# Forgetting attention and a bilinear FFN in one kernel: decay by a broadcast row and a DVE pass instead of by matmuls

## The chip, the cores and the metric

One core of a Trainium2 chip. The engines are TensorE (PE, with its weight loads as PEld), VectorE (DVE), ScalarE (ACT), GpSimd (POOL) and SyncE (SP), which issues most of the DMAs. The metric is device time in microseconds of one execution, the median of several runs. The profile is of one further execution.

## The reference

```python
# q, k, v: [8, 8, 576, 64]   f: [8, 8, 576]   fp32
scores = matmul(q, k^T) / sqrt(64)
log_f  = log(clip(f, 0.0001, 1.0))
cum    = cumsum(log_f, axis=-1)
decay  = cum[..., :, None] - cum[..., None, :]
scores = where(causal, -1e9, scores + decay)
attn   = softmax(scores)
x      = matmul(attn, v)         # then [8, 8, 576, 64] -> [4608, 512]
out    = ((x @ w_a) * (x @ w_b)) @ w_out     # w_a, w_b: [512, 1536], w_out: [1536, 512]
```

The term `cum[..., :, None]` is the same for a whole row, so the softmax takes it away again. Only `-cum[..., None, :]`, one value for each column, has to be added to the scores.

## The kernel before, in words

The work is a list of operations (class `Op`), each with an engine or several to choose from, a planned duration, what it depends on, a priority and the ring buffers that it takes. `schedule()` is a planner: it gives each operation an engine and a planned start, and the program is written out in that order. So each engine's queue has a fixed order, made when the kernel is built, and each waits in order for its semaphores.

Attention runs over `t`, a batch b (8) and a pair of heads pr (4), 32 in all. For a pair the queries come in blocks of 128 rows, `i` from 0 to 3, and a last one of 64 rows, `i` = 4, with both heads under each other in the 128 partitions. `groups = [(1, 0), (2,), (3,), (4,)]` says which blocks share a pair of PSUM banks (tile `sc`, two buffers).

For each pair:

- `qk_group` (matmuls at L463): q times k into `sc`; then the matrix `ones16` times `crs`, which adds the decay row: `crs` holds the row in two fp16 halves in two partitions per head; then `low` times `neg64`, the causal mask.
- `do_max` (L502, DVE): the negated maximum of each row of both heads of a block, from PSUM, into `st`.
- `do_exp` (L527, L531, ACT): the exponential of `sc` with that bias, from PSUM, into the fp16 tiles `PA` (blocks 0 to 2) and `PB` (blocks 3 and 4), with the row sum beside it.
- `do_recip` (L538, L540, DVE), then `do_norm` (L548, POOL): scaling of `PA` and `PB` by the reciprocal of the sum.
- `do_tr`: a DMA transpose of `PA` and `PB` on SP's queue (in batch 0 by PE and an eviction: `pe_tr`, L564), then `do_pv` and `do_pv4` (L588, L601, PE), then copies into `xT` (L608, L612, DVE).

`batch_inputs` loads q, k and v by head (L273, 256-byte pieces), casts them to fp16 (L265, L267; mostly on POOL from batch 1 on) and transposes q, k and the 64-row tail: with PE (`pe_path`, L300) for the batches in `PEB`, with DMA transposes for the others. `load_cr` loads `crs` of a batch from `cum_d`, a scratch in DRAM that was written once at the start.

`weights` loads the three weight matrices in 36 pieces of 128x512 fp32 into the ring `wl` by SP and casts each to fp16 on DVE or POOL (L451).

The FFN (`ffn`) follows in chunks of 512 tokens, two of 256 at the start: `psa` and `psb` (L732), a copy (L263, ACT), a product (L743, DVE), `pso` (L752), a copy (L263, L267) and a store (L762). A chunk needs the attention of all the batches that its tokens lie in; the planner puts the matmuls of earlier chunks between those of later pairs.

Of the kernel before, what the change touches and what calls it, by code (L numbers as in the profile page):

```python
# [25 lines left out]
def kernel(  # L26
# [34 lines left out]
    ones16 = perm.tile([128, 128], FP16, tag="ones16", name="ones16")  # L61
    cone = perm.tile([BH, S], FP16, tag="cone", name="cone")
# [3 lines left out]
    def constants():  # L66
        nc.gpsimd.memset(warm, 1.0)
        nc.gpsimd.memset(cone, 1.0)
        make_identity(nc, ident16)
        nc.gpsimd.memset(ones16, 0.0)  # L70
# [3 lines left out]
        for h in range(2):  # L74
            nc.gpsimd.memset(ones16[64 * h:64 * h + 2, :], 1.0)
            nc.gpsimd.affine_select(out=neg64[HP[h], :], in_=neg64[HP[h], :],
                                    compare_op=mybir.AluOpType.not_equal, fill=NEGBIG, base=0,
                                    pattern=[[-1, 64]], channel_multiplier=1)
            for half in range(2):
                x = low[half][HP[h], :]  # L80
                nc.gpsimd.affine_select(out=x, in_=x, compare_op=mybir.AluOpType.is_gt, fill=0.0,
                                        base=64 * half, pattern=[[-1, 128]], channel_multiplier=1)

    def paddings():
        for i in range(2):
            nc.gpsimd.memset(PB[i][:, 12, 64:128], 0.0)
            nc.gpsimd.memset(nv[i][64:128, NSB - 1, :, :], 0.0)
        nc.gpsimd.memset(crs[1], 0.0)
# [3 lines left out]
    wa16 = [perm.tile([128, DF], FP16, tag=f"wa16_{i}", name=f"wa16_{i}") for i in range(4)]  # L92
    wb16 = [perm.tile([128, DF], FP16, tag=f"wb16_{i}", name=f"wb16_{i}") for i in range(4)]
    wout16 = [perm.tile([128, DM], FP16, tag=f"wout16_{i}", name=f"wout16_{i}") for i in range(12)]
    nv = [perm.tile([128, NSB, H, D], FP16, tag=f"nv{i}", name=f"nv{i}") for i in range(2)]
    crs = [perm.tile([128, NP, S], FP16, tag=f"cr{i}", name=f"cr{i}") for i in range(2)]
    PB = [perm.tile([128, 13, 128], FP16, tag=f"PB{i}", name=f"PB{i}") for i in range(2)]

    RING = {"wl": 4, "n32": 4, "n16": 2, "n16t": 1, "nv": 2, "cr": 2, "qT": 2, "kT": 2, "tT": 2,
            "PA": 3, "PB": 2, "PTA": 3, "PTB": 2, "st": 6, "ht": 14, "a16": 3, "osb": 2,  # L100
            "sc": 2, "pv": 1, "ff": 3}
    wl_pool = pool("wl", RING["wl"])
# [9 lines left out]
    dram = pool("scr", 1, space=bass.MemoryType.DRAM)  # L112
# [7 lines left out]
    BACKLOG = 1.0  # L120
    PKT = {256: 0.021, 512: 0.031, 1024: 0.051, 2048: 0.095}

    class Op:


        def __init__(self, eng, dur, fn, deps=(), prio=0.0, land=None, mode=None, name="", bulk=False):
# [3 lines left out]
            self.bulk = bulk  # L130
# [12 lines left out]
    def schedule():  # L143
# [12 lines left out]
        def ready(o, e):  # L156
            t = 0.0
# [4 lines left out]
            for tag, _ in o.takes:  # L162
                lv = lives[tag]
                if len(lv) >= RING[tag]:
                    for u in lv[-RING[tag]]:
# [5 lines left out]
        while len(order) < len(ops):  # L171
            best = None
            for e, lst in pending.items():
                cand = None
                for o in lst:
# [3 lines left out]
                    at = max(r, free[e])  # L179
                    if o.bulk:  # L180
                        at = max(at, dma_free - BACKLOG)
                    if cand is None or at < cand[0] - 1e-9:
                        cand = (at, at + o.durs[e], o, e)
                        if at <= free[e] + 1e-9:
                            break
                if cand and (best is None or cand[0] < best[0] - 1e-9
# [11 lines left out]
            free[e] = at + dur  # L198
# [15 lines left out]
    T = {}  # L214


    cum_d = dram.tile([2, BH, S], FP16, tag="cum_d", name="cum_d")
    cw = {}

    def f_load(_):  # L220
        for n in ("f", "l", "c"):
            cw[n] = wl_pool.tile([128, 576], FP32, tag="wl", name=f"cum_{n}")
        cw["f"], cw["l"] = cw["f"][0:BH, 0:S], cw["l"][0:BH, 0:S]
        cw["c"] = cw["c"][0:BH, :].bitcast(FP16).rearrange("p (c s) -> p c s", c=2)
        nc.sync.dma_start(out=cw["f"], in_=f.rearrange("b h s -> (b h) s"))

    def warm_table(func):
# [3 lines left out]
    o_z = Op("DVE", 1.5, lambda _: nc.vector.memset(crs[0], 0.0), prio=-300)  # L231
    o_w = Op("ACT", 1.4, warm_table(LN), [], prio=-300)
    o_f = Op("SP", 0.55, f_load, prio=-300, land=0.6)
    wl_users = [take(o_f, "wl") for _ in range(3)]
# [4 lines left out]
        out=cw["f"], data0=cone, data1=cw["l"], initial=0.0, op0=MUL, op1=SUB), [o2], prio=-300)  # L239
    o4 = Op("DVE", 0.45, lambda _: nc.vector.tensor_copy(out=cw["c"][:, 0, :], in_=cw["f"]), [o3], prio=-300)  # L240
    o5 = Op("DVE", 0.75, lambda _: nc.vector.tensor_tensor(out=cw["c"][:, 1, :], in0=cw["f"],
                                                           in1=cw["c"][:, 0, :], op=SUB), [o4], prio=-300)
    o6 = Op("SP", 0.55, lambda _: nc.sync.dma_start(out=cum_d.rearrange("c r s -> r c s"), in_=cw["c"]), [o5],
            land=0.6, prio=-300)
    o_e = Op("ACT", 1.4, warm_table(EXP), [o2], prio=-300)
    for u in wl_users:
        u.extend([o1, o2, o3, o4, o5, o6])
# [4 lines left out]
    cr_op, cr_users, kq_users, kq_ops, tail_op, v_ops, v_users = {}, {}, {}, {}, {}, {}, {}  # L252
# [88 lines left out]
    def load_cr(b):  # L341
        for h in range(2):
            nc.sync.dma_start(
                out=crs[b % 2][64 * h:64 * h + 2, :, :],
                in_=cum_d[:, b * H:b * H + H, :].rearrange("c (p t) s -> t c p s", t=2)[h])
# [8 lines left out]
    PEB = (0, 1)  # L354
    PEP = (0,)

    def batch_inputs(b, base):
# [3 lines left out]
        o = Op("SP", 0.6, lambda _: load_cr(b), [o6, o_z] + ([o_p] if b else []) + gate(0), prio=base - 60, land=0.1)  # L361
        cr_users[b] = take(o, "cr")
        cr_op[b] = o
# [70 lines left out]
    def weights(base):  # L434
        items = []
        for j in range(3):
            for i in range(4):
                for nm, src, dst in (("a", moe_w_a, wa16), ("b", moe_w_b, wb16)):
                    cols = slice(512 * j, 512 * j + 512)
                    items.append(((nm, j), src[128 * i:128 * i + 128, cols], dst[i][:, cols]))  # L440
        for i in range(12):
            items.append((("o", i), moe_w_out[128 * i:128 * i + 128, :], wout16[i][:, :]))
        for n, (key, src, dst) in enumerate(items):
            def ld(_, n=n, src=src):
                T[("wl", n)] = wl_pool.tile([128, 576], FP32, tag="wl", name="wl")
                nc.sync.dma_start(out=T[("wl", n)][:, 0:512], in_=src)

            l = Op("SP", 0.55, ld, prio=base + 0.8 * n, land=packets(128, 2048), name=f"ldw{key[0]}{key[1]}", bulk=True)
            u = take(l, "wl")
            c = Op(None, {"DVE": 0.5, "POOL": 0.65},  # L450
                   lambda e, n=n, dst=dst: VEC[e].tensor_copy(out=dst, in_=T.pop(("wl", n))[:, 0:512]),  # L451
                   [l], prio=base + 0.8 * n, name=f"caw{key[0]}{key[1]}")
            u.append(c)
            w_ops.setdefault(key, []).append(c)


    def qk_group(t, g):
# [7 lines left out]
        if g == 3:  # L465
            for r in HP:
                mm(c[r, 0, :], tT[r, pr, 64:128], kT[r, 0:4, pr, :], start=True)
            for r in HP:
                mm(c[r, 1, 0:64], tT[r, pr, 64:128], tT[r, pr, 0:64], start=True)
            for bank, col, n in ((0, 0, 512), (1, 512, 64)):  # L470
                for r in HP:
                    mm(c[r, bank, 0:n], ones16[r, 0:64], crs[b % 2][r, pr, col:col + n], stop=(bank == 0))
# [12 lines left out]
        for i in groups[g]:  # L485
            for h, r in enumerate(HP):
                mm(c[:, h, pos[i]], ones16[r, :], crs[b % 2][r, pr, 0:128 * (i + 1)])
        for i in groups[g]:
# [7 lines left out]
    def do_max(t, i):  # L496
        key = ("st", t)
        if key not in T:
            T[key] = st_pool.tile([128, 32], FP32, tag="st", name="st")
        st = T[key]  # L500
        m = st[:, 8:9] if i == 4 else st[:, 2 * i:2 * i + 2]
        nc.vector.tensor_reduce(out=m, in_=T[("s", t, i)], axis=AXX, op=MAX, negate=True)  # L502
# [21 lines left out]
    def do_exp(t, i, h):  # L524
        st = T[("st", t)]
        if i == 4:
            nc.scalar.activation(out=p_blocks(t, 4), in_=T[("s", t, 4)], func=EXP, bias=st[:, 8:9],  # L527
                                 accum_out=st[:, 18:19])
            return
        c = 2 * i + h  # L530
        nc.scalar.activation(out=p_blocks(t, i)[:, :, h, :],  # L531
                             in_=T[("s", t, i)][:, h, :].rearrange("p (j k) -> p j k", k=128),
                             func=EXP, bias=st[:, c:c + 1], accum_out=st[:, 10 + c:11 + c])
# [81 lines left out]
    RED = {0: 0.42, 1: 0.69, 2: 0.955, 3: 1.22, 4: 0.75}  # L615
    EXPD = {0: 0.57, 1: 0.67, 2: 0.78, 3: 0.89, 4: 0.94}
    NORM = {0: 0.37, 1: 0.48, 2: 0.6, 3: 0.7, 4: 0.74}
    ev_ops = {}

    def attention(t, base):  # L620
# [7 lines left out]
        for g, gi in enumerate(groups):  # L628
            cols = sum(128 * (i + 1) for i in gi) if g < 3 else S
            m = min(g + 1, 3)  # L630
            deps = [kq_ops[(w, b, sb)] for w in "qk" for sb in range(m + 1)] + [cr_op[b], o_c]
            deps += [tail_op[b]] if g == 3 else []
            qk = Op("PE", (2 * cols + 128 * len(gi)) * COLS, lambda _, g=g: qk_group(t, g), deps,
                    prio=prio(g), mode="row", name=f"qk{t}.{g}")
            if g:
                qk.deps.append(qk_prev)
            qk_prev = qk
            qk_ops[(t, g)] = qk
            sc = take(qk, "sc")
            for u in (kq_users[("q", b)], kq_users[("k", b)], cr_users[b]) + ((kq_users[("t", b)],) if g == 3 else ()):  # L640
                u.append(qk)
            for i in gi:
                part = part_of(t, i)
                mx = Op("DVE", RED[i], lambda _, i=i: do_max(t, i), [qk], prio=prio(g), name=f"max{t}.{i}")
                if st_users is None:
# [219 lines left out]
```

## Time and profile before

| | |
|---|---|
| time, median of 3 runs | 451.19 us (450.91 to 453.85) |
| the profiled execution | 454.96 us, span 453.0 us |
| mean granted TensorE clock | 0.989 |
| POOL's last instruction | starts at 371.63 us (a group of 3, 2.09 us) |
| L502, DVE, row maxima | 160 instructions, 125.5 us |
| L463, PE, `ones16` times `crs` | 384 matmuls of 64 rows, six forms |
| L548, POOL, scaling of `PA` and `PB` | 192 and 96 instructions, 89.9 and 68.3 us |
| L451, casts of the weights | 36, on DVE and POOL |

The span runs from the first instruction to the last; what lies around it makes up the rest of the profiled execution's time. A line of groups names the line of the kernel, the engine, the operation, tile written and tiles read, count, busy time and mean nanoseconds of one, and then the engine's idle time in front of these instructions and who ended it. Matmuls on two halves of the array overlap, so their mean durations don't add up to PE's time.

### The profile page before, as it was taken

How to read it: one execution, taken by the hardware profiler on the slowest of the kernel's cores; microseconds unless marked ns; L12 is line 12 of the kernel's file. 1: busy time of each engine (PE TensorE's matmuls, PEld its weight loads, DVE VectorE, ACT ScalarE, POOL GpSimd, SP SyncE). 2: the span in 40 equal slices, each digit the busy share in tenths (PEclk: the TensorE clock that was granted, in tenths of full speed). 3: DMA queues.
4: the chain of work that ended last, by engine and by line, in shares of the span. 5: the costliest groups of instructions: out<-in, count | busy, mean ns of one | idle time of the engine just before them, and what ended most of it. 6: DMA issues, size and time to landing. Idle time of an engine off the chain costs nothing.

```text
span 453.0 us, 10430 instructions
## 1 busy us (share of the span) xinstructions
PE 423.6 (94%) x3868; PEld 217.4 (48%) x3868; DVE 275.5 (61%) x571; ACT 252.0 (56%) x739; POOL 230.9 (51%) x395
## 2 busy tenths in 40 slices
PE   2599985699999999999999999999999999999996
PEld 1456653466444444444544444444544544444442
DVE  6589867665777576656763677667656762331331
ACT  5468966564576657637662676567646661231320
POOL 6388879563757566728553676576556540000000
PEclk9999998799999999999999999999999999999999
DMA  8999999999999999999999999899997643101002
GB/s 160 212 266 255 258 256 209 213 215 204 220 198 182 198 214 196 180 216 200 200 186 222 201 200 197 191 209 205 182 208 160 94 88 86 46 1 69 24 1 93
DMA packets 242930, 78.32 MB, mean 173 GB/s; under 512 B 233344, under 2 KB 233600, under 8 KB 242880
## 3 DMA queue, kind: packets, MB, share of 16 engines
q1 hardware_dynamic: 242880, 77.67, 85.6%
q8 instruction: 30, 0.49, 0.4%
q14 instruction: 20, 0.16, 0.1%
HBM read 38.04 MB, written 9.58 MB: 105 GB/s over the span
## 4 chain that ended last, share of the span: by engine, by line
PE 85%; DVE 5%; DMA 4%; POOL 2%; ACT 1%; issue 1%; SPq 0%; POOLq 0%; DVEq 0%
PE pso L752 21%; PE psa L732 21%; PE psb L732 21%; PE sc L463 15%; PE pv L588 4%; DMA wl<-in_moe_w_out_dram 2%; DVE st L502 2%; PE pv L601 2%; DMA k<-in_k_dram 2%; POOL PA L548 1%; PE psT L300 1%; DVE wout L451 1%; ACT PA L531 1%; PE psP L564 1%; POOL PB L548 1%
## 5 line engine op out<-in xcount | busy, mean ns | idle before, releaser
L502 DVE TENSOR_REDUCE st<-sc 128x2 f32<-128x1024 f32 (+4 forms) x160 | 125.5, 805 | 39.9 <-PE sc L463 33.3
L548 POOL TENSOR_SCALAR PA<-PA,st 128x256 f16<-128x256 f16 (+2 forms) x192 | 89.9, 482 | 85.3 <-DVE st L540 76.5
L743 DVE TENSOR_TENSOR ht<-psb,a 128x512 f16<-128x512 f32 (+1 forms) x120 | 76.3, 636 | 64.4 <-PE psb L732 59.9
L732 PE MATMUL psa<-xT,wa 128*128 128x512 f16 (+1 forms) x480 | 114.0, 360 | 0.1
L531 ACT ACTIVATE PA<-sc,st 128x256 f16<-128x256 f32 (+2 forms) x192 | 89.5, 478 | 44.1 <-DVE st L502 29.5
L732 PE MATMUL psb<-xT,wb 128*128 128x512 f16 (+1 forms) x480 | 113.5, 359 | 0.1
L263 ACT CAST a<-psa 128x512 f16<-128x512 f32 (+1 forms) x120 | 65.2, 543 | 77.9 <-PE psa L732 77.3
L752 PE MATMUL pso<-wout,ht 128*128 128x512 f16 x432 | 101.9, 380 | 3.1 <-POOL wout L451 1.7
L548 POOL TENSOR_SCALAR PB<-PB,st 128x512 f16<-128x512 f16 (+1 forms) x96 | 68.3, 723 | 27.7 <-DVE st L540 15.9
L732 PEld LDWEIGHTS <-wa 128*128 128x128 f16 x480 | 43.6, 98 | 41.2 <-issue 0.6
L732 PEld LDWEIGHTS <-wb 128*128 128x128 f16 x480 | 43.5, 98 | 41.4 <-issue 0.3
L752 PEld LDWEIGHTS <-ht 128*128 128x128 f16 x432 | 39.0, 98 | 46.6 <-issue 3.5
L531 ACT ACTIVATE PB<-sc,st 128x512 f16<-128x512 f32 x64 | 43.7, 690 | 19.6 <-issue 6.9
L463 PE MATMUL sc<-cr,ones 64*128 64x256 f16 (+5 forms) x384 | 49.2, 308 | 0.0
L463 PE MATMUL sc<-kT,qT 64*128 64x128 f16 (+3 forms) x256 | 35.6, 316 | 4.6 <-ACT PB L531 2.5
L531 ACT ACTIVATION_READ_ACCUMULATOR PA<-sc,st 128x1 f32 x192 | 39.6, 206 | 0.0
L463 PEld LDWEIGHTS <-low 64*128 64x128 f16 (+1 forms) x576 | 24.6, 101 | 16.8 <-issue 2.0
L267 DVE COPY osb<-pso 128x512 f32<-128x512 f32 x18 | 12.4, 689 | 30.6 <-PE pso L752 30.6
L463 PE MATMUL sc<-neg,low 64*128 64x64 f16 (+1 forms) x576 | 31.0, 196 | 0.0
L608 DVE CAST xT<-pv 128x512 f16<-128x512 f32 (+1 forms) x36 | 22.6, 628 | 13.6 <-PE pv L588 13.6
L263 ACT COPY osb<-pso 128x512 f32<-128x512 f32 x18 | 10.5, 586 | 36.2 <-PE pso L752 34.2
L588 PEld LDWEIGHTS <-nv 128*64 128x64 f16 x640 | 20.3, 115 | 11.1 <-issue 9.0
(77 smaller groups left out, 344.5 us busy)
## 6 DMA issues: line engine op xcount, KB each, us to landing
out_dram<-osb SPq DMA_DIRECT2D x36, 256.0 KB, 2.2
k<-in_k_dram SPq DMA_DIRECT2D x32, 256.0 KB, 4.0
q<-in_q_dram SPq DMA_DIRECT2D x32, 256.0 KB, 4.2
v<-in_v_dram SPq DMA_DIRECT2D x32, 256.0 KB, 4.0
wl<-in_moe_w_a_dram SPq DMA_DIRECT2D x12, 256.0 KB, 3.8
wl<-in_moe_w_b_dram SPq DMA_DIRECT2D x12, 256.0 KB, 3.5
wl<-in_moe_w_out_dram SPq DMA_DIRECT2D x12, 256.0 KB, 4.7
t<-in_k_dram SPq DMA_DIRECT2D x8, 128.0 KB, 3.6
```

Of the source, the lines that this page charges most:

```text
L263: nc.scalar.copy(out=out_, in_=in_)
L267: VEC[e].tensor_copy(out=out_, in_=in_)
L463: nc.tensor.matmul(out=dst, lhsT=lhsT, rhs=rhs, start=start, stop=stop, skip_group_check=True)
L502: nc.vector.tensor_reduce(out=m, in_=T[("s", t, i)], axis=AXX, op=MAX, negate=True)
L531: nc.scalar.activation(out=p_blocks(t, i)[:, :, h, :], in_=T[("s", t, i)][:, h, :].rearrange("p (j k) -> p j k", k=128), func=EXP, bias=st ...
L548: VEC[e].tensor_scalar(out=p, in0=p, scalar1=st[:, c:c + 1], scalar2=1.0, op0=MUL, op1=MUL)
L588: nc.tensor.matmul(out=o[HP[h], 128 * i:128 * i + 128], lhsT=vt[:, j, 2 * pr + h, :], rhs=pt[:, base_blk[i] + 2 * j + h, :], start=first, ...
L601: nc.tensor.matmul(out=o[HP[h], 0:64], lhsT=vt[:, j, 2 * pr + h, :], rhs=pb[:, 8 + j, 64 * h:64 * h + 64], start=(j == 0), stop=(j == NSB ...
L608: nc.vector.tensor_copy(out=xT[pr][:, b, c], in_=T.pop(("pv", t, rows))[:, c])
L732: nc.tensor.matmul(out=p[:, 0:n], lhsT=w16[db][:, 128 * fb:128 * fb + 128], rhs=xTflat[db][:, t0:t0 + n], start=(db == 0), stop=(db == 3))
L743: nc.vector.tensor_tensor(out=ht[:, 0:n], in0=T.pop(("psb", t0, fb))[:, 0:n], in1=T.pop(("a16", t0, fb))[:, 0:n], op=MUL)
L752: nc.tensor.matmul(out=o, lhsT=T[("ht", t0, fb)][:, 128 * tb:128 * tb + 128], rhs=wout16[fb], start=(fb == 0), stop=(fb == 11))
```

## The change

The decay is no longer part of the matmuls. The cumulative sums stay in SBUF in fp32 (`cum`), and a batch's rows are copied to four partitions (`row`, one for each pair of heads). For each pair `spread` copies one row to all 128 partitions with GpSimd's `partition_broadcast` (tile `bc`, two buffers). `do_decay` takes the place of `do_max`: one DVE instruction for each block and head adds `sc` and `bc`, negates, writes the fp32 result to SBUF (tile `S`, two buffers) and takes the row minimum. The exponential then reads `S` with scale -1. In batch 0 the first group has broadcasts of its own, of 256 columns (`spread0`).

The weights come by nine DMAs on GpSimd's queue that cast while they copy, with a planned earliest start each. q, k and tail of batches 2 and 3 are transposed by PE too (`PEB`). The groups of a pair are multiplied two by two in one operation, except for the first two of batch 0. The planner picks PE's next operation with regard to the kind of matmul that ran last, counts a short tail of each instruction as free, and keeps bulk loads in order of priority.

```diff
-    ones16 = perm.tile([128, 128], FP16, tag="ones16", name="ones16")
-    cone = perm.tile([BH, S], FP16, tag="cone", name="cone")
+    cum = perm.tile([BH, S], FP32, tag="cum", name="cum")
...
-    RING = {"wl": 4, "n32": 4, "n16": 2, "n16t": 1, "nv": 2, "cr": 2, "qT": 2, "kT": 2, "tT": 2,
+    RING = {"S": 2, "bc": 2, "row": 1, "n32": 4, "n16": 2, "n16t": 1, "nv": 2, "qT": 2, "kT": 2, "tT": 2,
...
+    TAIL = {"DVE": 0.08, "ACT": 0.11, "POOL": 0.04}
+    W0, WD = 8, 5
...
+                    pick = now[0]
+                    if pick[0].mode != mode and mode != "full" and other:
+                        pick = (same or other)[0]
...
     o3 = Op("DVE", 1.35, lambda _: nc.vector.tensor_tensor_scan(
-        out=cw["f"], data0=cone, data1=cw["l"], initial=0.0, op0=MUL, op1=SUB), [o2], prio=-300)
-    o4 = Op("DVE", 0.45, lambda _: nc.vector.tensor_copy(out=cw["c"][:, 0, :], in_=cw["f"]), [o3], prio=-300)
-    o5 = Op("DVE", 0.75, lambda _: nc.vector.tensor_tensor(out=cw["c"][:, 1, :], in0=cw["f"],
-                                                           in1=cw["c"][:, 0, :], op=SUB), [o4], prio=-300)
-    o6 = Op("SP", 0.55, lambda _: nc.sync.dma_start(out=cum_d.rearrange("c r s -> r c s"), in_=cw["c"]), [o5],
-            land=0.6, prio=-300)
+        out=cum, data0=cw["1"], data1=cw["l"], initial=0.0, op0=MUL, op1=SUB), [o2, o0], prio=-300)
...
-    def load_cr(b):
-        for h in range(2):
-            nc.sync.dma_start(
-                out=crs[b % 2][64 * h:64 * h + 2, :, :],
-                in_=cum_d[:, b * H:b * H + H, :].rearrange("c (p t) s -> t c p s", t=2)[h])
+    def load_row(b):
+        T[("row", b)] = row_pool.tile([128, 2 * S], FP32, tag="row", name="row")
+        for t in range(2):
+            nc.sync.dma_start(out=T[("row", b)][0:128:32, t * S:t * S + S],
+                              in_=cum[b * H + t:b * H + t + 7:2, :])
...
-    PEB = (0, 1)
+    PEB = (0, 1, 2, 3)
...
-                nc.sync.dma_start(out=T[("wl", n)][:, 0:512], in_=src)
...
-            c = Op(None, {"DVE": 0.5, "POOL": 0.65},
-                   lambda e, n=n, dst=dst: VEC[e].tensor_copy(out=dst, in_=T.pop(("wl", n))[:, 0:512]),
-                   [l], prio=base + 0.8 * n, name=f"caw{key[0]}{key[1]}")
+            w_ops[key] = Op("POOL", 1.2, lambda _, src=src, dst=dst: nc.gpsimd.dma_start(out=dst, in_=src),
+                            prio=-250, land=packets(512, 2048), name=f"ldw{key[0]}{key[1]}")
+            w_ops[key].after = W0 + WD * n
...
         for i in groups[g]:
-            for h, r in enumerate(HP):
-                mm(c[:, h, pos[i]], ones16[r, :], crs[b % 2][r, pr, 0:128 * (i + 1)])
...
-        nc.vector.tensor_reduce(out=m, in_=T[("s", t, i)], axis=AXX, op=MAX, negate=True)
+    def spread(t):
+        b, pr = divmod(t, NP)
+        T[("bc", t)] = bc_pool.tile([128, 2 * S], FP32, tag="bc", name="bc")
+        nc.gpsimd.partition_broadcast(T[("bc", t)], T[("row", b)][32 * pr:32 * pr + 1, :], channels=128)
+
+    def spread0(t):
...
+        for h in range(2):
+            nc.gpsimd.partition_broadcast(T[("bc0", t)][:, 512 * (t % 2) + 256 * h:512 * (t % 2) + 256 * h + 256],
+                                          T[("row", 0)][32 * t:32 * t + 1, S * h:S * h + 256], channels=128)
+
+    def do_decay(t, g, i, h):
...
+        nc.vector.tensor_tensor_reduce(out=o, in0=x, in1=y, scale=-1.0, scalar=3e38, op0=ADD, op1=MIN, accum_out=m)
...
         nc.scalar.activation(out=p_blocks(t, i)[:, :, h, :],
-                             in_=T[("s", t, i)][:, h, :].rearrange("p (j k) -> p j k", k=128),
-                             func=EXP, bias=st[:, c:c + 1], accum_out=st[:, 10 + c:11 + c])
+                             in_=T[("z", t, i)][:, h * n:h * n + n].rearrange("p (j k) -> p j k", k=128),
+                             func=EXP, scale=-1.0, bias=st[:, c:c + 1], accum_out=st[:, 10 + c:11 + c])
...
+        bc = Op("POOL", 1.35, lambda _: spread(t), [row_op[b], o_c], prio=prio(1) - 12, name=f"bc{t}")
...
+        for gs in ([(0,), (1,), (2, 3)] if b == 0 else [(0, 1), (2, 3)]):
```

## The prediction

> **What bounds the kernel now.** I read the busy shares, then the 40 slices, then the chain that ended last, and from there the stage that holds most of the time.
>
> ```profile
> span 453.0 us, 10430 instructions
> PE 423.6 (94%) x3868; PEld 217.4 (48%) x3868; DVE 275.5 (61%) x571; ACT 252.0 (56%) x739; POOL 230.9 (51%) x395
> PE   2599985699999999999999999999999999999996
> POOL 6388879563757566728553676576556540000000
> PE 85%; DVE 5%; DMA 4%; POOL 2%; ACT 1%; issue 1%; SPq 0%; POOLq 0%; DVEq 0%
> ```
>
> PE is the bound: 94% busy, 85% of the last chain, full from the tenth slice on. What it loses lies in the first 95 us. POOL is at half load and stops at slice 33, so in this kernel it has room. How much room, the windows tell, here first POOL alone in the first 20 us, then all engines in the steady stage (us, then busy time of PE, PEld, DVE, ACT, POOL, with the instructions):
>
> ```profile
> 0.00:20.00 20.00, 9.23 (x29) 1.00 0.91 181
> ```
>
> ```profile
> 120.00:200.00 80.00, 80.00 (x780) 38.42 (x778) 53.27 (x111) 50.09 (x156) 46.56 (x77) 1.00 1.09 194
> ```
>
> In the steady stage PE has no gap in 80 us, DVE 27 us free, POOL 33.
>
> **The change on POOL.** This is where I look for the end, so it comes first. Each head pair t gets one broadcast of 128x1152 words (spread), batch 0 eight small ones besides (spread0): 40 in all. In the GpSimd queue of the changed program an instruction that asks for a set of routines stands ahead of them: set 1 before a broadcast, set 0 again before the next scaling (do_norm). I count 33 requests for set 1 and 34 for set 0, nearly strictly in turn, two for each t. The kernel before has one request, for set 0, at the mask helper, between these two lines of POOL's timeline:
>
> ```profile
> 1.34 0.20 POOL masks.py:197 MEMSET ident<- 128x128 f16 x1
> 1.61 0.29 POOL masks.py:199 TENSOR_SCALAR_AFFINE_SELECT ident<-ident 128x128 f16<-128x128 f16 x1
> ```
>
> The memset ends at 1.54, the next starts at 1.61: asking for a set that, it seems, was there already cost at most 0.07 us. Asking for the other set is in no row. 66 requests do that (67 less the first).
>
> What a real switch costs has to be bounded. Below by 0.07 us, if the request never does anything. [...]
>
> ```profile
> k<-in_k_dram SPq DMA_DIRECT2D x32, 256.0 KB, 4.0
> wl<-in_moe_w_out_dram SPq DMA_DIRECT2D x12, 256.0 KB, 4.7
> v<-in_v_dram SPq DMA_DIRECT2D x8, 128.0 KB, 6.1
> cum_d<-cum_c SPq DMA_DIRECT2D x1, 144.0 KB, 2.5
> ```
>
> My upper end is twice the longest, 12.2 us. The ends are far apart. [...]
>
> [...]
>
> POOL's other work, from its groups:
>
> ```profile
> L548 POOL TENSOR_SCALAR PA<-PA,st 128x256 f16<-128x256 f16 (+2 forms) x192 | 89.9, 482 | 85.3 <-DVE st L540 76.5
> L548 POOL TENSOR_SCALAR PB<-PB,st 128x512 f16<-128x512 f16 (+1 forms) x96 | 68.3, 723 | 27.7 <-DVE st L540 15.9
> L267 POOL CAST k<-k 128x1024 f16<-128x1024 f32 x14 | 14.5, 1036 | 1.7 <-DMA k<-in_k_dram 1.7
> ```
>
> - Scalings stay: 89.9 + 68.3 = 158.2 us.
> - Casts: k 14.5, q 14 of 1.044 us and one of 0.62, v 14 of 1.038 and 8 of 0.603, tails 7 of 0.602 and 7 of 0.616: 57.5. The 16 weight casts (10.2 us) go.
> - Constants: last start 5.80 plus 0.52, less some 1.1 for the memsets that go: 5.3. The memset of crs[1] (2.02) goes.
> - Nine casting weight DMAs now issue on POOL. No row; between SP's shortest issue in the trace (0.33) and POOL's longest instruction (2.02), so 3 to 18 us in all; I take one 1024-wide cast each, 9.4.
> - Broadcasts: no row. At the pace of the 1024-wide cast 1152 words are 1.17 us; 32 of them 37.4, and 8 of 256 words at the 484 ns of a 256-wide scaling 3.9: 41.3. Ends: 24 (the 576-wide scaling's 752 ns each) to 65 (2.02 each).
>
> Sum without switches 271.7 us.
>
> **What of it lies on the path.** With 7.2 us a switch POOL needs 271.7 + 66 x 7.2 = 747 us, PE under 424: POOL sets the pace. Queued behind a switch on POOL's queue are the scalings of PA and PB, the next batch's casts of k, q, v and tail, and the weight DMAs. Behind those wait: SP's transposes of PA and PB, then PE's pv, then DVE's copies to xT and the FFN; behind a broadcast wait DVE's decay passes, then ACT's exponentials. Scores stay two buffers (sc) and the broadcast rows two (bc), so the others can run ahead by about a pair and no further. POOL's idle time of before, 373.7 - 230.9 = 143 us up to its last instruction, is mostly waits of one or two us for reciprocals; a switch in front of each segment of some eight scalings gives DVE and ACT 14 us lead per pair, so I let these vanish. I keep the idle time of the first 20 us, 20 - 9.23 = 10.8; the ends are 0 and 143.
>
> After POOL's last scaling comes a tail. Before, by POOL's timeline and the chain (start, us, what):
>
> ```profile
> 371.63 2.09 POOL L548 TENSOR_SCALAR PB<-PB,st 128x512 f16<-128x512 f16 x3 [0.94 <-DVE st L540]
> ```
>
> ```profile
> 379.79 0.68 PE pv L588 x20
> ...
> 381.71 5.29 PE pso L752 x24
> ```
>
> From 373.7 to the end at 453.0 are 79.3 us: 6.1 until pv (transpose), then two chunks of the FFN and the store. Of it 0.97 + 5.29 are backlog of an earlier chunk, which a waiting PE has done long before: 73.0.
>
> Span: 271.7 + 10.8 + 475.2 + 73.0 = 830.7. The profiled execution took 454.96 for a span of 453.0 (1.96 around it) and stands 3.8 us over the runs' median of 451.19, so 830.7 + 1.96 - 3.8 = **829 us**.
>
> **The other parts, which POOL then hides.** PE: the cr/ones products go. In the steady stage their pairs take 0.16 (groups 0 and 1 of i), 0.17, 0.22 and 0.24 us by the starts of the next group, 0.79 for each t, 25.3 over 32. PE transposes of q, k and tail for batches 2 and 3 come: 72 at 0.97 us per eight, 8.7. Net -16.6. SP: 36 weight loads, the cum_d store, 16 cr loads and six q/k/tail transposes go, 16 row loads come; the queue has more room. DVE: L502 by columns is 0.148 us plus 1.047 ns each (416 ns for 256, 1220 for 1024). Two passes per block give 0.282, 0.416, 0.550, 0.684, and 0.754 for the last, doubled 5.37 us for each t against 4.03: +43. Each pass has a read of the accumulated minimum behind it, 320 in all; no DVE row, between 0 and a reciprocal's 154 ns: 0 to 49 us. Weight casts on DVE (20, 13.9 us) and half of the q/k evictions (some 6) about cancel. ACT reads S in SBUF instead of scores in PSUM, so sc comes free after DVE's pass; a 512-wide ACT cast takes 617 ns from SBUF (k) and 586 from PSUM (psa), so 288 exponentials at +0.03 are +9 us. DVE at 310 to 360 us and ACT at 261 stay under POOL's 747. If POOL's cover is gone, PE gains the 16.6 and DVE, at 53 of 80 us now, comes near its full load.
>
> **Rivals.**
> - A, a request for a set is as cheap as the one row (0.07 us). For it: the only request measured. Against: that one asked for what was there. Then POOL needs 272 of the time and PE stays the bound: 451.2 - 16.6 = 435 us; 424 if the waits for wout in the first 95 us (4.89 and 5.61 on the chain) also go, 455 if DVE's accumulator reads all cost 154 ns and its queue fills. POOL decides from 355.5 - 1.8 + 66x = 451.2, x = 1.5 us a switch: above that the change is slower. This is the case on the other side.
> - B, only set 1 is fetched and set 0 stays in place, as the 0.07 may mean: 33 x 7.2 = 238, 591 us.
> - C, a switch is two full transfers at the longest row, 12.2 us: 66 x 12.2 = 805, 1159 us. For it: DMA engines are 0.9 to 1.1 busy before. Against: over a longer run they thin out.
>
> **How the numbers follow.** Forecast 0.70, A 0.10, B 0.09, C 0.11. The forecast's own range is 4.0 us (one k load) to 9.4 (two of 4.7) a switch: 618 to 974. With B and C taken in: 590 to 1160; A is left out. A measurement of this kernel tells about 1% from no change. Faster by over 1% is A without its bad end, 0.09; same 0.01; slower 0.90.
>
> **What will show it.** POOL idle with no releaser before the first broadcast and the first scaling after it, some 7 us each, 66 times; POOL busy near 272 us all the same, for a request need not show as work; PE idle in most slices up to the last tenth; DVE waiting for bc or sc; last POOL scaling some 73 us before the end. Broadcast rows near 1.2 us, accumulator reads as DVE rows of their own, no cr/ones rows. Wrong, if those gaps are under 1.5 us: then PE is full again and the time is near 435. Gaps only before broadcasts would be B; gaps of 12 us C.

## The result and the profile after

The changed kernel takes 847.71 us (median of 4 runs, 844.67 to 849.88) against 452.52 us before (4 runs on the same chip, 450.91 to 454.44): a ratio of 1.8725, 95% interval 1.8612 to 1.8838. The forecast was 829 us, with a range of 590 to 1160.

First the same lines of the page as shown of the kernel before: span, busy shares, the 40 slices of PE and POOL, and the chain that ended last.

```profile
span 842.8 us, 10464 instructions
...
PE 456.6 (54%) x3556; PEld 230.5 (27%) x3556; DVE 308.1 (37%) x1051; ACT 254.5 (30%) x728; POOL 271.4 (32%) x422
...
PE   2216452443413546694097534690496545719998
...
POOL 4312332333333333333243233433142334232000
...
PE 23%; issue 17%; DMA 8%; POOL 8%; DVE 4%; SPq 1%; POOLq 0%; ACT 0%; DVEq 0%
```

No engine is busy for more than 54% of the span. A reader of the first lines alone would say that nothing bounds this kernel. POOL is busy 271.4 us, 40 more than before, and yet its row of slices is the evenest: two or three tenths nearly everywhere, until it stops in the 37th slice and PE runs nearly full. On the chain a word has come up that was at 1% before: "issue", 17%, time in which an engine waited for nothing that the profile shows. The steady stage says the same (us, busy time of PE, PEld, DVE, ACT, POOL, granted clock, DMA share, GB/s):

```profile
120.00:200.00 80.00, 38.84 (x403) 26.81 (x400) 28.93 (x102) 20.21 (x63) 30.63 (x43) 0.73 0.41 79
```

PE was at 80.00 of 80 there, the DMA engines at 1.09; now they are at 38.84 of 80 and at 0.41. Who waits for whom is in the view of waits (engine, line, waited for: us in total, times, longest). First POOL's, then PE's:

```profile
POOL bc L503 <- issue: 123.2, 20, 7.2
POOL PB L582 <- issue: 114.6, 16, 8.9
POOL PA L582 <- issue: 106.7, 15, 10.5
POOL PA L582 <- DVE st L574: 31.4, 11, 6.6
```

```profile
PE pv L622 <- DMA PTB<-PB: 158.3, 16, 18.0
PE psP L598 <- POOL PA L582: 44.0, 8, 17.5
PE psT L317 <- POOL k L284: 33.2, 3, 15.8
```

PE waits for the transposes of `PB`, for scalings and for casts: all of it work that stands on POOL's queue behind a request for a set of routines, or one DMA behind that. POOL waits for "issue". POOL's timeline around one pair shows what such a wait is (start, length, what, and in brackets the idle time in front of it):

```profile
399.58 1.04 POOL L282 TENSOR_SCALAR q<-q 128x1024 f16<-128x1024 f32 x1
406.55 1.43 POOL L503 PARTITION_BROADCAST bc<-row  x1 [5.93 <-issue]
415.17 2.08 POOL L582 TENSOR_SCALAR PB<-PB,st 128x512 f16<-128x512 f16 x3 [7.19 <-issue]
417.23 1.03 POOL L282 TENSOR_SCALAR q<-q 128x1024 f16<-128x1024 f32 x1
```

A broadcast of 1.43 us stands between two gaps, 5.93 us before it and 7.19 us behind it. No row shows work in them, and there is none at the same place between the scaling and the cast that follow. Followed through the whole timeline, from each last scaling or cast to the broadcast behind it and from there to the next instruction with a request for the other set ahead of it, there are 33 gaps of each kind: 206.3 us ahead of broadcasts (median 5.99) and 240.2 on the way back (median 7.10), together 446.6 us, 6.77 each. The lines of the view of waits above hold most of them; where an instruction of another engine, mostly DVE, ended within such a gap, the view names that instruction instead. POOL's last instruction ends at 768.25 us, 74.5 us before the span does.

The start of the kernel shows that the gap goes with the change and not with the broadcast. There the eight small broadcasts of batch 0 follow each other, with one DMA issue between them, and only the first has a gap:

```profile
14.67 2.62 POOL L510 PARTITION_BROADCAST bc<-row  x6 [8.43 <-issue]
17.13 0.94 POOL L462 DMA_DIRECT2D wb<-in_moe_w_b_dram  x1
18.11 1.23 POOL L510 PARTITION_BROADCAST bc<-row  x2
```

### The profile page after: what moved, and what is told of

It is laid out like the page before. It is cut to its first block, busy times and chain, and to the rows that moved or that the text cites. A ratio compares the mean times of both kernels' runs of the same rounds, so it can differ in the third digit from the quotient of the medians.

```text
span 842.8 us, 10464 instructions
## 1 busy us (share of the span) xinstructions
PE 456.6 (54%) x3556; PEld 230.5 (27%) x3556; DVE 308.1 (37%) x1051; ACT 254.5 (30%) x728; POOL 271.4 (32%) x422
## 3 DMA queue, kind: packets, MB, share of 16 engines
q1 hardware_dynamic: 228112, 65.72, 39.0%
## 4 chain that ended last, share of the span: by engine, by line
PE 23%; issue 17%; DMA 8%; POOL 8%; DVE 4%; SPq 1%; POOLq 0%; ACT 0%; DVEq 0%
PE pso L817 8%; PE psb L797 6%; PE psa L797 6%; DMA PTB<-PB 6%; POOL PB L582 3%; POOL bc L503 2%; DVE S L536 2%; PE sc L473 2%; POOL PA L582 2%; PE pv L622 2%; DMA q<-in_q_dram 1%; DVE ht L808 1%; DMA row<-cum 1%; PE pv L635 1%; DMA qT<-q 1%
## 5 line engine op out<-in xcount | busy, mean ns | idle before, releaser
L536 DVE CUSTOM_DVE_ANT_0 S<-sc,bc 128x512 f32<-128x512 f32 (+4 forms) x320 | 160.7, 536 | 74.3 <-POOL bc L503 40.7
L565 ACT ACTIVATE PA<-S,st 128x256 f16<-128x256 f32 (+2 forms) x192 | 95.5, 499 | 178.0 <-DVE st L536 177.7
L797 PE MATMUL psb<-xT,wb 128*128 128x512 f16 (+1 forms) x480 | 125.8, 389 | 0.0
L797 PE MATMUL psa<-xT,wa 128*128 128x512 f16 (+1 forms) x480 | 124.6, 386 | 0.2
L817 PE MATMUL pso<-wout,ht 128*128 128x512 f16 x432 | 112.0, 412 | 0.0
L622 PE MATMUL pv<-PTB,nv 128*64 128x128 f16 x256 | 25.1, 272 | 158.3 <-DMA PTB<-PB 158.3
L503 POOL PARTITION_BROADCAST bc<-row x32 | 45.7, 1429 | 197.9 <-issue 123.2
L565 ACT ACTIVATE PB<-S,st 128x512 f16<-128x512 f32 x64 | 46.0, 719 | 97.5 <-DVE st L536 40.9
L622 PE MATMUL pv<-PTA,nv 128*64 128x128 f16 x384 | 30.2, 264 | 29.5 <-DMA PTA<-PA 28.3
L565 ACT ACTIVATION_READ_ACCUMULATOR PA<-S,st 128x1 f32 x192 | 36.2, 189 | 0.0
L280 ACT COPY osb<-pso 128x512 f32<-128x512 f32 x18 | 10.5, 585 | 84.0 <-PE pso L817 74.0
```

Of the source, the lines that this page charges most:

```text
L280: nc.scalar.copy(out=out_, in_=in_)
L503: nc.gpsimd.partition_broadcast(T[("bc", t)], T[("row", b)][32 * pr:32 * pr + 1, :], channels=128)
L536: nc.vector.tensor_tensor_reduce(out=o, in0=x, in1=y, scale=-1.0, scalar=3e38, op0=ADD, op1=MIN, accum_out=m)
L565: nc.scalar.activation(out=p_blocks(t, i)[:, :, h, :], in_=T[("z", t, i)][:, h * n:h * n + n].rearrange("p (j k) -> p j k", k=128), func=E ...
L622: nc.tensor.matmul(out=o[HP[h], 128 * i:128 * i + 128], lhsT=vt[:, j, 2 * pr + h, :], rhs=pt[:, base_blk[i] + 2 * j + h, :], start=first, ...
L797: nc.tensor.matmul(out=p[:, 0:n], lhsT=w16[:, db, 128 * fb:128 * fb + 128], rhs=xTflat[db][:, t0:t0 + n], start=(db == 0), stop=(db == 3))
```

## The experiments

The theory of the prediction is that each change of POOL's set of routines costs some 7 us in which POOL stands, and that POOL then sets the pace. Its rivals afterwards were that the broadcast itself, the new DVE passes or the new transfers cost the time.

**No switch.** The broadcasts become zero fills on POOL; one request for a set is left in its queue, at the start.

```diff
-        nc.gpsimd.partition_broadcast(T[("bc", t)], T[("row", b)][32 * pr:32 * pr + 1, :], channels=128)
+        nc.gpsimd.memset(T[("bc", t)], 0.0)
```

> The broadcasts on GpSimd are replaced by fills of the same tiles with zero (the decay is left out of the scores); queue orders stay, and no set of routines is asked for any more but set 0 at the start. Theory S (the 66 switches between the two sets, 5.9 us idle before a broadcast and 7.0 before the next scaling in the changed kernel's trace, set the time): POOL needs about 260 us, PE is the bound again, 435 us, at most 455. Rival P (the merged score groups, the in-order queues and the lower granted clock of 0.787 cost much of it by themselves): 550 us or more, with a clock that stays under 0.9. Rival W (the work of the broadcasts, 1.43 us each, and the wait for the row are what costs): 435 too, so this run does not tell W from S.

Measured: 439.37 us (437.67 to 440.99), ratio 0.9682, interval 0.9624 to 0.974. The steady stage:

```profile
120.00:200.00 80.00, 80.00 (x762) 38.99 (x760) 62.50 (x221) 54.18 (x157) 56.14 (x89) 1.00 1.07 193
```

Of POOL's waits for "issue" this is the largest line left:

```profile
POOL PA L581 <- issue: 5.2, 2, 2.6
```

PE is full again, with the DVE passes, the nine cast DMAs, the row copies and all else in place, and POOL busy 256.4 us. So the whole loss, and more than all of it, hangs on the 40 broadcasts. The rest of the change is worth about 3%.

**Switches alone, in the kernel before.** One broadcast of a single column for each pair, whose output nobody reads, ahead of the scaling of block 2.

```diff
+        if i == 2 and h == 0:
+            nc.gpsimd.partition_broadcast(many, one[0:1, :], channels=128)
```

> The kernel before with one broadcast of a single word to 128 partitions added on GpSimd for each pair of heads, ahead of the first scaling of block 2; nobody waits for it. 64 switches, and nothing else of the change. Theory S: POOL 231 + 64 x 6.5 = 647 us of work and switching, some tens of us of waits and the tail of 79 us: 740 to 810. Rival W: 32 broadcasts of under 1 us in POOL's free time, 452 us. Rival P: 452 us, since no other part of the change is there.

Measured: 810.5 us (one run), span 808.8. The time lies at the upper end of the 740 to 810 us that the theory gave. The 32 broadcasts take 0.28 us each, 9.0 in all, and nothing reads what they write; the view puts a single wait of 1.1 us down to them. POOL's waits:

```profile
POOL many L548 <- issue: 175.9, 28, 8.0
POOL PA L553 <- issue: 149.3, 21, 7.8
```

In these two lines a gap is 6.28 us ahead of a broadcast and 7.11 on the way back. The span grew by 355.8 us for 64 switches, 5.6 each; the rest of a switch falls into idle time that POOL had before. This takes decay passes, row copies and the broadcasts' own length out of the case.

**Half of the switches.** The broadcasts of the odd pairs become zero fills; the even pairs keep theirs.

> The changed kernel with the broadcast of each odd pair replaced by a fill with zero (the decay is left out there); the eight small broadcasts of batch 0 stay. 34 switches in place of 66. Theory S: 32 x 6.5 = 210 us less, 635 us (600 to 660). Rival P: within some tens of us of 848. Rival W: 16 broadcasts less, 16 x (1.43 - 1.0) = 7 us less.

Measured: 646.81 us (one run), span 645.1. Spans of 436.7, 645.1 and 842.8 us for 0, 34 and 66 switches: 208.4/34 = 6.13 and 197.7/32 = 6.18 us a switch. By these three kernels the time is a straight line in the number of switches.

**The rows by DMA.** If the switch is the fault, the rows have to come another way. Here SP copies each from DRAM to all 128 partitions, 576 KB for a pair.

```diff
-        nc.gpsimd.partition_broadcast(T[("bc", t)], T[("row", b)][32 * pr:32 * pr + 1, :], channels=128)
+        nc.sync.dma_start(out=T[("bc", t)],
+                          in_=cum_d[2 * t:2 * t + 2, :].rearrange("h s -> (h s)").partition_broadcast(128))
```

> The decay row comes to the 128 partitions by DMA from a copy of the cumulative sums in DRAM instead of by GpSimd (40 DMAs on SP's queue, 590 KB each for the 32 large ones, three buffers); the rest of the change stays, and no switch is left. Theory S: near the run with fills, 435 us (425 to 460), 19 MB more to move in 4.6 KB pieces. If it beats the kernel before, the other parts of the change were worth the 16.6 us of PE that the prediction gave them. Rival P: 550 or more. Rival W: the same as S.

Measured: 515.63 us (513.38 to 517.1), ratio 1.1373, interval 1.1299 to 1.1448: a miss. The page's line of the queue that SP feeds (packets, MB, share of 16 engines) and the stage:

```profile
q1 hardware_dynamic: 233760, 85.64, 84.1%
```

```profile
120.00:200.00 80.00, 71.23 (x635) 35.92 (x635) 57.29 (x201) 47.61 (x141) 45.41 (x76) 0.87 1.11 210
```

I had looked at POOL and DVE and not at the queue: the DMA engines were at 1.09 in this stage before, and this queue now moves 85.64 MB, where it moves 65.72 in the changed kernel. PE gets 71 of 80 us. My reading is that the row copies only trade one bound for another; the next run, which spreads the rows without these bytes, is the test of it.

**The rows by DVE.** A row goes by an 18 KB DMA into four partitions, one in each group of 32, and one `stream_shuffle` on DVE spreads it within each group. No set is changed, and few bytes move.

```diff
+        nc.sync.dma_start(out=T[("bc", t)][0:128:32, :],
+                          in_=cum_d[2 * t:2 * t + 2, :].rearrange("h s -> (h s)").partition_broadcast(4))
...
+        nc.vector.stream_shuffle(out=x, in_=x, mask=[0] * 32)
```

> The changed kernel with the decay row put into partitions 0, 32, 64 and 96 by a DMA of 18 KB from DRAM and spread inside each 32 partitions by one DVE shuffle of 1152 words for each pair (512 words for each pair's first group in batch 0); three buffers; GpSimd does no broadcast and asks for no other set. Theory S: near the run with fills (439 us), with 32 x 1.3 + 4 x 0.65 = 44 us more on DVE (307 to 351 us of 440) and 36 less on POOL: 440 us (432 to 455), faster than before. If DVE becomes the bound: 455 or more, with DVE over 95% in the steady stage. That the DMA broadcast ran at 516 us would then be due to its 19 MB, of which this run moves 0.6.

Measured: 451.78 us (449.07 to 454.69, 10 runs), ratio 0.9974, interval 0.9946 to 1.0002: the loss is gone, and with 0.6 MB of rows in place of 19 the time is 64 us shorter than with the rows by DMA. But 12 us of the zero fills' gain are missing. Two windows of it, then the same two of the zero-fill kernel:

```profile
0.00:20.00 20.00, 4.11 (x36) 2.61 (x36) 10.40 (x28) 6.58 (x15) 10.45 (x27) 1.00 1.10 200
120.00:360.00 240.00, 236.59 (x2096) 114.05 (x2095) 208.09 (x699) 161.28 (x471) 141.90 (x239) 0.98 1.01 188
```

```profile
0.00:20.00 20.00, 6.83 (x78) 4.79 (x79) 10.57 (x42) 9.81 (x30) 11.32 (x37) 1.00 1.11 196
120.00:360.00 240.00, 237.04 (x2177) 114.28 (x2174) 188.88 (x676) 162.66 (x479) 164.60 (x263) 1.00 1.00 187
```

In the steady stage PE is about equally busy in both, though DVE carries 208 of 240 us. At the start the shuffle version is behind: PE has done 15.2 us of work in the first 40, the zero fills 23.3 (in the kernel before 25.4). There the sums first go to DRAM (4.1 us) and come back (4.7) before the first shuffle. These 8.1 us are two thirds of the 12.4 between the two spans. The rest comes later: 0.5 us of idle time of PE in the steady stage, 2.5 after 360 us, and 1.5 more of PE's busy time over the whole span, at a mean clock of 0.973 against 0.975. The 95 to 120 us stretch costs both about 8 us (PE 16.8 of 25, against 25.00 before), after a gain of 6 between 40 and 95 (50 of 55, against 44.07).

**The other two parts, each alone in the kernel before.** The nine weight DMAs that cast, in place of 36 loads and 36 casts; then the PE transposes of q, k and tail for batches 2 and 3 (`PEB = (0, 1, 2, 3)`).

> The kernel before with the weights by nine cast DMAs on GpSimd's queue, with the planned starts of the change; nothing else. By the chain of before, 10.5 us of waits for wout (4.89 and 5.61) can go: 442 us. If the nine loads only push the loads of q, k and v back: 453 (same) or slower. 440 to 456.

> The kernel before with q, k and tail of batches 2 and 3 transposed by PE; nothing else. PE is the bound, so 72 transposes at 0.121 us more: 453 + 8.7 = 461 us, slower. If the DMA transposes were what the steady stage waits for: 453 or less.

Measured: 457.95 us for the weight DMAs, ratio 1.0091 (1.0064 to 1.0118), a miss: a loss where I expected a gain. 455.92 us for the transposes, ratio 1.0055 (1.003 to 1.0079): a loss, but 2.4 us rather than 8.7. With the cast DMAs PE is busy only 3.06 of the first 20 us (7.50 before), and its longest wait is one for the decay rows' first load:

```profile
PE sc L456 <- DMA cr<-cum_d: 8.8, 1, 8.8
```

The sums reach that load by way of DRAM. In the kernel before the store is issued at 9.5 us and the load at 12.1; here at 9.4 and 16.2, and three of the 512 KB weight DMAs are issued between 8.3 and 10.7. The large transfers and the delay of the small ones fall together; no run took them apart. In exchange the waits of 40 to 95 us go (54.72 of 55 against 44.07), but 9 us come back at 95 to 120. Alone, then, neither part gains.

**Shuffle without the two batches' PE transposes** (`PEB = (0, 1)` in the shuffle version).

> The same with q, k and tail of batches 2 and 3 transposed by DMA again, as before the change (PEB of two batches). If PE is the bound in the steady stage: 8.7 us less than the run with PEB of four batches, some 432 us. If the DMA queues are (share 1.0 in the run with fills): the same or slower.

Measured: 461.65 us, ratio 1.0161 (1.0095 to 1.0228): a miss, and in the other direction. PE has 224.04 us of work in the 240 of the steady stage, against 236.59, at a DMA share of 1.05. Once PE is relieved of the decay products, the transfers look like the next limit, and the transposes that move from DMA to PE pay: 10 us here, where they cost 2.4 in the kernel before.

**A faster start and a lighter DVE.** Two versions of the shuffle with rows copied once for a batch, from SBUF to SBUF, eight copies of 9 KB each; the second has the copies of `pv` into `xT` on ACT too.

```diff
+                nc.sync.dma_start(out=rowp[32 * c:32 * c + 4, t * S:t * S + S],
+                                  in_=cum[b * H + t:b * H + t + 7:2, :])
...
+        nc.vector.stream_shuffle(out=T[("bc", t)], in_=rowp, mask=[pr] * 32)
```

> The version without switches by a shuffle (e5) spends its 12 us over the zero-fill version at the start: the cumulative sums go to DRAM (4.1 us), come back as a row (4.7 us), and only then comes the shuffle. Here the rows of a batch go once, from SBUF to SBUF, to four partitions of each quarter (8 small copies for a batch), and each pair's shuffle picks its own partition. If the two transfers in a row at the start are the cause, one of them goes: 4 to 6 us less than e5, 445 to 448, faster than before by 1 to 1.5%. If DVE's load (87% in the steady stage) is the cause, or the 64 copies on SP's queue take back what is won, 450 to 453, no change.

> The same with the copies of pv into xT (512 columns, 32 of them at 0.63 us) on ACT in place of DVE. If DVE's load holds PE up in the steady stage, another 2 to 4 us less than the version with rows alone; if only the start counts, within 1 us of it, or a little more, since a copy then waits behind an exponential.

Measured: 474.44 us, ratio 1.047 (1.0442 to 1.0497), and 464.98, ratio 1.0263 (1.023 to 1.0296). The first is a plain miss: PE's first 20 us are no better (3.68 us busy), and in the steady stage PE falls to 222.51 of 240. The second edit is worth 9.5 us here, more than the 2 to 4 expected; PE's windows place 2.7 of it in the first 40 us and 1.5 in the steady stage (223.99 of 240), and no run shows where the rest comes from. So the steady stage, not the start, is what this way of copying loses. The next two runs ask what the `xT` edit gives in the version without these copies, and whether the single row tile is their fault.

> The shuffle version e5 with the 512-column copies of pv into xT on ACT in place of DVE (nothing else). In the version with row copies this edit was worth 465.0 against 474.4 us. If DVE's load in the steady stage (87%) is what the shuffle version loses, 441 to 447, faster than before by 1 to 2%. If its loss lies at the start alone, 449 to 452, no change.

> The row version with the copies on ACT (e10) and two row tiles in place of one. If e9 and e10 lost their time because the row copies of the next batch wait on SP's queue until the last shuffle of a batch has read the one tile, and hold the transposes behind them, 443 to 452. If the 64 small copies themselves are the loss (3 us of SP's queue for each batch), 460 to 466 as before.

Measured: with the copies on ACT the shuffle version takes 449.73 us (five runs from 446.64 to 451.47, one at 453.35) against 453.36 before, ratio 0.99, interval 0.9861 to 0.9938. That lies in the range expected for a loss at the start alone, 449 to 452; it is a small gain all the same. It is the fastest version with the whole computation, faster than before by 1.0% and than the changed kernel by almost half. PE has 238.50 of 240 us in the steady stage where it had 236.59. Two row tiles: 463.33 us, ratio 1.0198 (1.0161 to 1.0236), 1.6 us better than with one (464.98). So the one tile is at most a small part of the loss. SP's timeline has this line in that kernel:

```profile
201.75 5.52 SPq L363 DMA_DIRECT2D rowp<-cum  x8
```

The eight issues hold SP's queue for 5.5 us here, with the next transposes of `PA` and `PB` behind them; the 18 KB loads of the other version stand apart, at 0.6 to 0.8 us each in the same stretch. That this is the loss fits the run, but no run took it away by itself, so it stays open.

## Why the prediction was right, point by point

- **The mechanism.** POOL stands at each change of set, 6.77 us in the mean and twice for each pair, with scalings, casts and weight DMAs queued behind it; PE, busy 54% of the span, waits for those. The zero fills, the half and the switches alone all say so.
- **The price of a switch** was taken as 7.2 us, my estimate: the times of two transfers of the kernel before, 4.7 and 2.5 us, added up. No run shows that term, nor that a switch is made of transfers. What the trace shows in its place is idle time: a median of 5.99 ahead of a broadcast and 7.10 on the way back, 446.6 us for the 66, where the sum had 475.2: 28.6 too many. The two ends are not alike, which the prediction did not provide for. That 7.2 came near the mean of 6.77 is partly luck, for no row shows what goes on in a gap. None of the 66 changes came cheap: the shortest gap is 5.73 us.
- **POOL's other idle time** was taken as 10.8 us. POOL is idle 768.25 - 271.4 = 496.9 us until its last instruction ends; less 446.6, 50.3 remain, 39.5 too few in the sum. The first 20 us are idle for 10.3 us, as said, but 8.4 of that is the gap ahead of the first broadcast, which the sum had counted as a switch already; nearly all of the 50.3 comes later. The failed step is "I let these vanish": the lead of DVE and ACT does not cover every wait for a reciprocal (31.4 us in 11 waits of the `PA` scalings for L574 alone, none of them in one of the 66 gaps), and one wait for a load of the tail (`t`) adds 7.3.
- **POOL's work**: 271.7 forecast, 271.4 measured. The broadcasts were sized too small (1.43 us, not 1.17; 45.7 and 3.8 us in all, not 37.4 and 3.9). The cast-DMA issues took 8.3 us where 9.4 were taken, the scalings 155.3 against 158.2, and neighbouring rows overlap by some 4 us. So the agreement of the total to 0.3 us is luck.
- **The tail**: 73.0 forecast, 74.5 measured. The sum of the terms, 830.7, is 12 us short of the span of 842.8: 28.6 too many for the switches, 39.5 and 1.5 too few for idle time and tail, 0.3 too many for work. The two large misses have opposite signs, so the forecast is nearer to the time than its terms are to theirs.
- **DVE.** The passes were forecast at 282, 416, 550, 684 and 754 ns; the groups, each shape apart, have 284, 419, 549, 680 and 751. The read of the accumulated minimum, bounded by 0 and 154 ns, takes 83. DVE's total of 308.1 us lies just under the 310 to 360 forecast, ACT's 254.5 under 261; neither set the time.

```profile
L536 DVE CUSTOM_DVE_ANT_0 S<-sc,bc 64x576 f32<-64x576 f32 x64 | 48.1, 751 | 0.8
L536 DVE CUSTOM_DVE_ANT_0 S<-sc,bc 128x512 f32<-128x512 f32 x64 | 43.1, 680 | 3.8 <-PE sc L473 3.5
...
L536 DVE CUSTOM_DVE_ANT_0 S<-sc,bc 128x256 f32<-128x256 f32 x64 | 25.1, 419 | 53.2 <-POOL bc L503 24.3 <-PE sc L473 15.0 <-POOL PB L582 11.6
L536 DVE DVE_READ_ACCUMULATOR2_ANT st<- 128x1 f32 x256 | 21.2, 83 | 0.0
```

- **PE.** A net 16.6 us less was forecast; without the switches PE is busy 399.6 us against 423.6, 24.0 less. One mis-sized term is the 72 PE transposes for 8.7 us: alone in the kernel before they add 4.5 us of busy time (428.1) and 2.4 of time. The other 3.2 us stay open: no run takes the cr products (25.3) out alone, and the weight DMAs alone, with the same 3868 matmuls as before, already change PE's busy time by 5.1 us (418.5).
- **The rivals.** A (a request costs nothing) falls with the gaps, though its time of 435, range 424 to 455, is what the zero fills gave (439). That time was built on PE's 16.6 us, and the span with the zero fills is 16.3 shorter than before. The agreement is luck: PE has 24.0 us less to do there, but is idle for 7.7 more (37.1 against 29.4). Its point of decision, 1.5 us a switch, lies far under what was measured. B (only set 1 is fetched) falls with the 7.1 us on the way back, and C (12.2 us) with the longest gap of all, 10.5.

## What to carry to other kernels

Before a new operation goes on GpSimd's queue, count how often the queue changes its set of routines: here each change held it for 6 to 7 us, twice for every lone broadcast of 1.4 us. An operation that another engine can do (here a DVE shuffle of 1.5 us behind an 18 KB load) was the better choice: 452 us, or 450 with copies moved to ACT, where the broadcasts took 848. Another way would be all broadcasts together, so that the set changes once; the eight at the start share one gap, but no run tried it for the rest. And when no engine is busy for much more than half of the span, look for the one whose gaps say "issue": here a busy share of 32% hid that POOL set the pace.

## What the runs showed of the hardware that was not expected

- The two directions of a switch differ: 30 of the 33 gaps ahead of a broadcast lie between 5.7 and 6.7 us, 30 of the 33 on the way back between 6.8 and 7.4. The longest, 8.4 to 10.5 us, are among the first four of each kind.
- The granted TensorE clock fell to 0.787 in the mean with PE at half load, and to 0.73 in the stage where PE is busy 38.84 of 80 us; in the stages shown with PE busy for 80.00 of 80 us it is 1.00. In the first 40 us of the changed kernel PE is busy for 11.5 us only, and there the clock is 1.00: in this trace not every stretch of low load has a low clock. The kernel with switches alone shows 0.775, the half 0.851, the zero fills 0.975. So PE's 456.6 us of busy time are no sign of more work: the zero fills run the same 3556 matmuls in 399.6.
- A `stream_shuffle` of 128x1152 fp32 took 1.47 us on DVE in the shuffle version (mean of 32), about as long as the broadcast's 1.43 on GpSimd.
